# Half of the third exponential tile added in place by GpSimd, six key buffers with spread loads, and late tiles gated after head group six

## The chip, the cores and the metric

The kernel runs on one core of one Trainium2 chip. The metric is the device time of one execution in microseconds, lower being better. Inside the core five engines work side by side, each through its own instructions in order, held together by semaphores: TensorE (PE, matmuls; PEld is its weight load), VectorE (DVE), ScalarE (ACT), GpSimd (POOL) and SyncE (SP), which here issues nearly all DMA transfers. POOL issues a few transfers itself, and makes their descriptors in software.

## The reference

With `xn` the layer norm of `x` (2048 rows of 512, bfloat16), the result is `x + s * silu(b)`:

- `s` is attention with 32 heads of width 128 over given keys and values (2048 each): `q = xn @ wq`, `p = softmax(q @ k.T / sqrt(128))`, `o = p @ v`, and the heads' outputs side by side times `wo`.
- `b` is a two-layer mixer: gelu of a layer norm times `w1`, its quarters shifted by one or two rows, times `w2`, added to `xn`; then a gelu MLP of width 1792 over a second layer norm.

## The kernel before

A first stage (to about 118 us) does the layer norms, the mixer and half of its MLP; `silu(b)`, the **gate**, is kept in DRAM in tiles of 128 rows. The attention follows, and takes nearly all of the time.

The attention is cut into 128 **units**, numbered 0 to 127 here: one head for one block of 512 queries. The order is: head group `g` (eight groups of four heads), then query block `qt` (four), then head `hh` in the group. A group thus has 16 units; unit `16*g + 4*qt + hh`. A unit has eight **slots** `p`, numbered through as `n = 8*u + p`. In each slot (`s_slot`, L432) PE multiplies two chunks of 128 keys by the 512 queries into `ps_s`, and ACT takes the exponential of both (128 x 1024, L443) into half of a tile `pT`; a unit fills four such tiles, `pT[0]` to `pT[3]`. The product with the values (`pv_slot`, L475) comes 10 slots later. The rest of a unit is woven into the slots: query projections for units ahead (`product`, L374, in Strassen's form for pairs of units, finished by DVE in L420 to L428), and output projections (`wo_product`, L569, in Strassen's form for groups 1 to 5, `wo_mm`, L611, for the others).

The softmax's denominators are DVE's work. For unit `u`:

- slot 4: `add_first` (L449): `acc = pT[0] + pT[1]`, 128 x 2048, both inputs in SBUF.
- slot 6: for units in `APART` (L1046, units 24 to 109) POOL adds the two halves of `pT[2]` into a tile `ph` (`add_aside`, L455, 128 x 1024). For other units DVE adds the whole of `pT[2]` into `acc` (`add_next`, L465, 128 x 2048).
- slot 0 or 1 of the next unit: `add_last` (L1092): in `APART` DVE adds `ph` into the lower half of `acc` (`add_join`, L460), then in every unit `pT[3]` into `acc` (L465); two folds follow (L469, L473).
- slot 3 of the next unit: SP transposes the folded row block (`tT<-acc`, L498). One unit on, DVE sums it (L503) and takes the reciprocal (L509); SP writes that to DRAM (`dr<-rc`, L511) and reads it back on all partitions (`rb<-dr`, L515); DVE then scales the unit's output from PSUM by it (`oT`, L527), which frees the PSUM bank.

All of these transfers stand in SP's one queue with the loads. `load_k` (L140) loads a head's keys in four pieces of 512 keys by a transposing DMA (L145), `load_v` (L149) its values in two. There are five key buffers and five value buffers. `at(n, fn)` (L135) hangs a call on slot `n`; the main loop (L1123) runs what is due at the end of the slot. L985 to L994 set the loads of the next group's heads: with `b` the group's unit 12, key pieces go two to a unit, in slots 5 and 6, from unit `b - 2` to `b + 6`.

The output sums over heads stand in SBUF per tile of 128 rows, `sacc[t]` (16 tiles; `t // 4` is the query block). **Late** tiles are those of query blocks 2 and 3. In group 6 they are turned from sums of `wo` into sums of the final result: `gate_load` fetches the gate (L600), `y_scale` multiplies the sum by half the gate (L629, DVE, both inputs in SBUF), `y_add` adds `x` by an accumulating DMA on POOL's queue (L633). L1080 to L1085 hang these on units 104 to 111 (scale at slot 3, POOL's DMA at slot 5). From then on each product for a late tile is gated before it is added: `wo_post` (L646) makes `tm = 0.5 * ps * gate` (L655) and adds it (L658) in group 6; in group 7 `y_out` (L635) adds and writes. Tiles of blocks 0 and 1 are finished within `wo_post` (L662 to L669). `wo_join` (L593) folds a sum that Strassen's form kept apart into the tiles, L1078 sets when. DVE's order is the program's order: `pin` keeps it.

Of the kernel before, what the change touches and what calls it, by code (L numbers as in the profile page):

```python
# [17 lines left out]
def kernel(  # L18
# [15 lines left out]
    nc = tc.nc  # L34
    P = nc.NUM_PARTITIONS
# [3 lines left out]
    Sq, D = x2d.shape  # L39
    _, H, Sk, Dh = A_k_cache.shape  # L40
# [10 lines left out]
    HG = 4  # L51
# [83 lines left out]
    def at(n, fn):  # L135
        todo[n].append(fn)
# [3 lines left out]
    def load_k(h, pieces):  # L140
        w = Sk // KSPLIT
        for i in pieces:
            if i == 0:
                kTs[h] = kp.tile([P, Sk], BF16, name="kT")
            pin(nc.sync.dma_start(  # L145
                out=kTs[h][:, i * w:(i + 1) * w],
                in_=A_k_cache[0, h, i * w:(i + 1) * w, :], transpose=True))

    def load_v(h, halves):  # L149
        v = A_v_cache[0, h].rearrange("(i p j) d -> p i j d", p=P, j=KJ)  # L150
        for i in halves:
            if i == 0 and h == H - 1:
                vX[0] = vp.tile([P, KC, Dh + 2], BF16, tag="vb", name="vx")
                pin(nc.vector.memset(vX[0][:, :, Dh:Dh + 1], 1.0))
                vBs[h] = vX[0][:, :, 0:Dh]
            elif i == 0:
                vBs[h] = vp.tile([P, KC, Dh], BF16, tag="vb", name="vb")
            w = KSPLIT // 2
            dst = vBs[h].rearrange("p (i j) d -> p i j d", j=KJ)
            for ks in [slice(i * w, (i + 1) * w)] if h < H - 1 else range(i * w, (i + 1) * w):  # L160
                pin(nc.sync.dma_start(out=dst[:, ks], in_=v[:, ks]))

    def load_w(h, eng=nc.sync):
        wqs[h] = wqp.tile([P, DC, Dh], BF16, name="wq_h")
# [2 lines left out]
    vX = {}  # L167
# [281 lines left out]
        pin(nc.vector.tensor_tensor(  # L449
            out=s["acc"][:], in0=s["pT"][0][:], in1=s["pT"][1][:], op=ALU.add))  # L450

    def add_aside(u):
        s = st[u]
        s["ph"] = pS.tile([P, 2, 512], BF16, tag="tm", bufs=2, name="ph")
        pin(nc.gpsimd.tensor_tensor(  # L455
            out=s["ph"][:], in0=s["pT"][2][:, 0:2, :], in1=s["pT"][2][:, 2:4, :], op=ALU.add))

    def add_join(u):
        a = st[u]["acc"]
        pin(nc.vector.tensor_tensor(  # L460
            out=a[:, 0:2, :], in0=a[:, 0:2, :], in1=st[u].pop("ph")[:], op=ALU.add))

    def add_next(u, i):
        a = st[u]["acc"]
        pin(nc.vector.tensor_tensor(out=a[:], in0=a[:], in1=st[u]["pT"][i][:], op=ALU.add))  # L465
# [73 lines left out]
    def halves(x):  # L539
        return x.rearrange("p (a c) -> p a c", a=2)  # L540
# [87 lines left out]
    def y_scale(t):  # L628
        pin(nc.vector.scalar_tensor_tensor(  # L629
            out=sacc[t], in0=sacc[t], scalar=0.5, in1=halves(gin[t]), op0=ALU.mult, op1=ALU.mult))  # L630

    def y_add(t):
        pin(nc.gpsimd.dma_start(out=sacc[t], in_=halves(xsrc[t]), accum_op=ALU.add))  # L633

    def y_out(t, tm, queue):  # L635
        y = token(False, "y")
        pin(nc.vector.tensor_tensor(out=halves(y[:]), in0=halves(tm[:]), in1=sacc[t], op=ALU.add))
        pin(queue.dma_start(out=out2d[t * P:(t + 1) * P, :], in_=y[:]))

    owed = deque()  # L640
# [5 lines left out]
    def wo_post(g, t, n):  # L646
        ps = wo_box.pop(0)
        if g == 0:
            sa_open(t)
            pin(nc.vector.tensor_copy(out=sacc[t], in_=halves(ps[:])))  # L650
            return
        sa = sacc[t]
        if t // 4 in LATE:
            tm = pS.tile([P, D], FP32, tag="tm", bufs=2, name="tm")
            pin(nc.vector.scalar_tensor_tensor(  # L655
                out=tm[:], in0=ps[:], scalar=0.5, in1=gin[t], op0=ALU.mult, op1=ALU.mult))
            if g < NG - 1:
                pin(nc.vector.tensor_tensor(out=sa, in0=sa, in1=halves(tm[:]), op=ALU.add))  # L658
# [7 lines left out]
        pin(nc.vector.scalar_tensor_tensor(
            out=halves(gl), in0=sa, scalar=0.5, in1=halves(gl), op0=ALU.mult, op1=ALU.mult))
        pin(nc.vector.tensor_tensor(out=xl[:], in0=gl, in1=xl[:], op=ALU.add))
        pin(nc.sync.dma_start(out=out2d[t * P:(t + 1) * P, :], in_=xl[:]))  # L669

# [452 lines left out]
    for n in range(UB * SPU):  # L1123
# [234 lines left out]
```

## Time and profile before

| what | us |
|---|---|
| three runs | 1226.6, 1231.92, 1233.73 (median 1231.92) |
| the profiled execution | 1233.66 |
| its span, first to last instruction | 1231.9 |
| PE busy | 1214.8 |
| ACT busy | 1106.2 |
| DVE busy | 1087.9 |
| POOL busy | 244.2 |
| granted TensorE clock, mean | 0.999 |

What lies around the span is 1233.66 - 1231.9 = 1.76 us. Matmuls are pipelined in the profile, so a busy PE is not a PE at its peak; the windows of single units say more than the share of the whole. "Idle before, with releaser" in a timeline is the time that an engine stood still ahead of an instruction, and the instruction or transfer that ended it.

### The profile page before, as it was taken

How to read it: one execution, taken by the hardware profiler on the slowest of the kernel's cores; microseconds unless marked ns; L12 is line 12 of the kernel's file. 1: busy time of each engine (PE TensorE's matmuls, PEld its weight loads, DVE VectorE, ACT ScalarE, POOL GpSimd, SP SyncE). 2: the span in 40 equal slices, each digit the busy share in tenths (PEclk: the TensorE clock that was granted, in tenths of full speed). 3: DMA queues.
4: the chain of work that ended last, by engine and by line, in shares of the span. 5: the costliest groups of instructions: out<-in, count | busy, mean ns of one | idle time of the engine just before them, and what ended most of it. 6: DMA issues, size and time to landing. Idle time of an engine off the chain costs nothing.

```text
span 1231.9 us, 18553 instructions
## 1 busy us (share of the span) xinstructions
PE 1214.8 (99%) x6469; PEld 667.1 (54%) x6591; DVE 1087.9 (88%) x1891; ACT 1106.2 (90%) x1241; POOL 244.2 (20%) x185
## 2 busy tenths in 40 slices
PE   9999999999999999999999999999999999899998
PEld 7466444455555555555555555555555555455545
DVE  7853778999999999999989999999998899899997
ACT  6345999899999999999999999999999999899996
POOL 5300000000023222223223222223232333200000
PEclk9999999999999999999999999999999999999999
DMA  8671224454344523453244423552334345553432
GB/s 181 168 154 51 48 52 76 96 104 82 69 82 104 112 48 78 100 104 77 75 90 100 102 52 82 102 109 60 78 91 103 83 88 114 116 119 66 91 96 68
DMA packets 248157, 113.05 MB, mean 92 GB/s; under 512 B 195328, under 2 KB 231296, under 8 KB 248064
## 3 DMA queue, kind: packets, MB, share of 16 engines
q1 hardware_dynamic: 244560, 107.21, 41.2%
q0 software_dynamic: 2944, 4.20, 1.6%
q8 instruction: 51, 0.84, 0.3%
q14 instruction: 42, 0.34, 0.2%
q10 hardware_dynamic: 560, 0.46, 0.1%
HBM read 69.60 MB, written 4.45 MB: 60 GB/s over the span
## 4 chain that ended last, share of the span: by engine, by line
PE 83%; DVE 12%; DMA 3%; issue 2%; ACT 0%; POOL 0%; DVEq 0%
PE ps_s L112 35%; PE ps_o L112 31%; PE ps_q L112 7%; PE ps_wo L112 7%; PE ps_m L112 3%; DVE acc L465 2%; DVE acc L449 2%; DVE oT L527 1%; DVE sm L503 1%; DMA rb<-dr 1%; DMA dr<-rc 1%; DMA tT<-acc 1%; DVE acc L473 1%; DVE acc L469 1%; DVE sacc L658 0%
## 5 line engine op out<-in xcount | busy, mean ns | idle before, releaser
L443 ACT ACTIVATE pT<-ps_s 128x1024 bf16<-128x1024 f32 x1016 | 1015.6, 1028 | 56.3 <-PE ps_s L112 25.3
L112 PE MATMUL ps_s<-qT,kT 128*128 128x512 bf16 (+1 forms) x2057 | 608.4, 378 | 4.3 <-DVE qT L428 3.7
L112 PE MATMUL ps_o<-pT,vb 128*128 128x512 bf16 x1889 | 569.9, 379 | 4.4
L455 POOL TENSOR_TENSOR ph<-pT 128x1024 bf16<-128x1024 bf16 x86 | 200.2, 2328 | 625.8 <-ACT pT L443 600.8
L112 PEld LDWEIGHTS <-vb 128*128 128x128 bf16 x1984 | 193.8, 98 | 217.5 <-issue 1.5
L112 PEld LDWEIGHTS <-kT 128*128 128x128 bf16 x2064 | 230.8, 113 | 95.3 <-DVE qT L428 5.2
L465 DVE TENSOR_TENSOR acc<-acc,pT 128x2048 bf16<-128x2048 bf16 x168 | 204.4, 1217 | 19.5 <-ACT pT L443 13.6
L449 DVE TENSOR_TENSOR acc<-pT 128x2048 bf16<-128x2048 bf16 x127 | 157.6, 1241 | 11.3 <-ACT pT L443 11.2
L527 DVE TENSOR_TENSOR oT<-ps_o,rb 128x512 bf16<-128x512 f32 x127 | 86.7, 683 | 14.7 <-DMA rb<-dr 14.0
L591 DVE TENSOR_TENSOR sacc<-ps_wo,sacc 128x512 f32<-128x512 f32 (+1 forms) x160 | 97.0, 606 | 0.5 <-PE ps_wo L112 0.5
L112 PE MATMUL ps_wo<-wo_h,oT 128*128 128x512 bf16 (+1 forms) x330 | 91.7, 327 | 1.6 <-DVE tm L655 0.6
L503 DVE TENSOR_REDUCE sm<-tT 128x4 f32<-128x512 bf16 x124 | 84.0, 677 | 6.5 <-DMA tT<-acc 5.8
L469 DVE TENSOR_TENSOR acc<-acc 128x1024 bf16<-128x1024 bf16 x127 | 87.3, 687 | 2.5
L112 PEld LDWEIGHTS <-wc 128*128 128x128 bf16 x440 | 43.0, 98 | 52.5 <-issue 0.8
L112 PEld LDWEIGHTS <-oT 128*128 128x128 bf16 x448 | 43.5, 98 | 47.9 <-issue 0.9
L112 PEld LDWEIGHTS <-wq_h 128*128 128x128 bf16 x398 | 39.0, 98 | 46.7 <-issue 0.6
L112 PE MATMUL ps_q<-xnT,wq_h 128*128 128x256 bf16 (+1 forms) x284 | 60.3, 298 | 0.3
L460 DVE TENSOR_TENSOR acc<-acc,ph 128x1024 bf16<-128x1024 bf16 x86 | 58.6, 681 | 2.0 <-POOL ph L455 1.9
L298 ACT ACTIVATE h2T<-ps_s 128x1024 bf16<-128x1024 f32 x28 | 28.6, 1022 | 31.6 <-PE ps_s L112 31.6
L473 DVE TENSOR_TENSOR acc<-acc 128x512 bf16<-128x512 bf16 x127 | 53.4, 421 | 2.5
L112 PEld LDWEIGHTS <-so 128*128 128x128 bf16 x320 | 31.3, 98 | 38.6 <-issue 1.2
L112 PEld LDWEIGHTS <-w_sb 128*128 128x128 bf16 x368 | 33.6, 98 | 29.1
(134 smaller groups left out, 903.7 us busy)
## 6 DMA issues: line engine op xcount, KB each, us to landing
rb<-dr SPq DMA_DIRECT2D x127, 256.0 KB, 3.9
vb<-in_A_v_cache_dram SPq DMA_DIRECT2D x62, 256.0 KB, 3.0
wq_h<-in_A_wq_dram SPq DMA_DIRECT2D x32, 128.0 KB, 2.8
wo_h<-in_A_wo_dram SPq DMA_DIRECT2D x32, 128.0 KB, 2.3
w_sb<-in_B_w_dram SPq DMA_DIRECT2D x8, 256.0 KB, 4.7
kT<-in_A_k_cache_dram SPq DMA_TRANSPOSE x128, 2.7
gate<-xall POOLq DMA_DIRECT2D x16, 128.0 KB, 2.3
sacc<-in_A_x_dram POOLq DMA_DIRECT2D x8, 256.0 KB, 4.3
```

What stands on the lines that cost most here:

```text
L112: pin(nc.tensor.matmul(out=out, lhsT=lhsT, rhs=rhs, start=start, stop=stop, **kw))
L298: pin(nc.scalar.activation(out=h2[c][:, f], in_=ps[:], func=ACT.Gelu_apprx_tanh))
L443: pin(nc.scalar.activation(out=s["pT"][-1][:, jj:jj + 2, :], in_=sps[:], func=ACT.Exp, scale=SCALE))
L449: pin(nc.vector.tensor_tensor(out=s["acc"][:], in0=s["pT"][0][:], in1=s["pT"][1][:], op=ALU.add))
L455: pin(nc.gpsimd.tensor_tensor(out=s["ph"][:], in0=s["pT"][2][:, 0:2, :], in1=s["pT"][2][:, 2:4, :], op=ALU.add))
L460: pin(nc.vector.tensor_tensor(out=a[:, 0:2, :], in0=a[:, 0:2, :], in1=st[u].pop("ph")[:], op=ALU.add))
L465: pin(nc.vector.tensor_tensor(out=a[:], in0=a[:], in1=st[u]["pT"][i][:], op=ALU.add))
L469: pin(nc.vector.tensor_tensor(out=a[:, 0:2, :], in0=a[:, 0:2, :], in1=a[:, 2:4, :], op=ALU.add))
L473: pin(nc.vector.tensor_tensor(out=a[:, 0, :], in0=a[:, 0, :], in1=a[:, 1, :], op=ALU.add))
L503: pin(nc.vector.tensor_reduce(out=sm[:], in_=s["tT"][:], axis=mybir.AxisListType.X, op=ALU.add))
L527: pin(nc.vector.tensor_tensor(out=to, in0=o, in1=rb, op=ALU.mult))
L591: pin(nc.vector.tensor_tensor(out=out, in0=ps, in1=out, op=ALU.add))
```

## The change

It has these parts:

- **The third tile.** In `APART`, POOL adds the lower half of `pT[2]` straight into the lower half of `acc` (slot 6), and DVE adds the upper half into the upper half (in `add_last`). `ph` is gone. The shapes (128 x 1024) stay.
- **`APART`** now runs from unit 24 to 124.
- **Keys.** Heads with `h % 6 == 5` have a key buffer of their own (tag `kx`, in the place of `ph` and `tm`), so there are six. The pieces of the first head of a group are loaded one a unit from `b - 10`, those of the second from `b - 6`, those of the third and fourth from `b + 1` to `b + 6`. Values move up by one slot, those of a group's first head by one unit.
- **Late tiles.** Gate loads, scales and POOL's adds of `x` move from units 103 to 111 to units 112 to 121, one tile a unit; POOL's DMA now stands at slot 6, behind POOL's add. In group 6 a late tile's product is added plainly (one DVE instruction less for each of eight tiles). `tm` of group 7 takes a key buffer.
- **Order.** The last two steps of tiles of blocks 0 and 1 (`y_last`) wait for slot 3 of a next unit; four `wo_join` pairs move up by four to five units.

PE's instructions and their order stay as they are; DVE has eight instructions fewer.

```diff
-            if i == 0:
-                kTs[h] = kp.tile([P, Sk], BF16, name="kT")
+            if i == 0 and h % (HG + 2) == HG + 1:
+                kTs[h] = pS.tile([P, Sk], BF16, tag="kx", bufs=1, name="kT")
+            elif i == 0:
+                kTs[h] = kp.tile([P, Sk], BF16, tag="kT", name="kT")
...
-    def add_aside(u):
-        s = st[u]
-        s["ph"] = pS.tile([P, 2, 512], BF16, tag="tm", bufs=2, name="ph")
-        pin(nc.gpsimd.tensor_tensor(
-            out=s["ph"][:], in0=s["pT"][2][:, 0:2, :], in1=s["pT"][2][:, 2:4, :], op=ALU.add))
-
-    def add_join(u):
-        a = st[u]["acc"]
-        pin(nc.vector.tensor_tensor(
-            out=a[:, 0:2, :], in0=a[:, 0:2, :], in1=st[u].pop("ph")[:], op=ALU.add))
+    def add_half(u, eng, part):
+        a, e = st[u]["acc"], st[u]["pT"][2]
+        pin(eng.tensor_tensor(out=a[:, part, :], in0=a[:, part, :], in1=e[:, part, :], op=ALU.add))
...
-        if t // 4 in LATE:
-            tm = pS.tile([P, D], FP32, tag="tm", bufs=2, name="tm")
+        if t // 4 in LATE and g == NG - 1:
+            if t % 2 == 0:
+                pair[0] = kp.tile([P, 2, D], FP32, tag="kT", name="tm")
+            tm = pair[0][:, t % 2, :]
             pin(nc.vector.scalar_tensor_tensor(
-                out=tm[:], in0=ps[:], scalar=0.5, in1=gin[t], op0=ALU.mult, op1=ALU.mult))
-            if g < NG - 1:
-                pin(nc.vector.tensor_tensor(out=sa, in0=sa, in1=halves(tm[:]), op=ALU.add))
-            else:
-                owed.append((t, tm))
+                out=tm, in0=ps[:], scalar=0.5, in1=gin[t], op0=ALU.mult, op1=ALU.mult))
+            owed.append((t, tm))
             return
         pin(nc.vector.tensor_tensor(out=sa, in0=halves(ps[:]), in1=sa, op=ALU.add))
-        if g < NG - 1:
-            return
+        if g == NG - 1:
+            last.append(t)
...
-            for i in range(KSPLIT):
-                at((b - 2 + (2 * hh + i // 2 + (hh > 0))) * SPU + (5, 6)[i % 2], lambda h=h, i=i: load_k(h, (i,)))
+            for i, u in enumerate(((-10, -9, -8, -7), (-6, -5, -2, -1) if g else (-4, -3, -2, -1), (1, 1, 2, 3), (4, 5, 5, 6))[hh]):
+                at((b + u) * SPU + 5, lambda h=h, i=i: load_k(h, (i,)))
             for i in range(2):
-                at((b - 1 + (2 * hh + i + (hh > 0))) * SPU + 7, lambda h=h, i=i: load_v(h, (i,)))
+                at((b + (-2, 2, 4, 6)[hh] + i) * SPU + 6, lambda h=h, i=i: load_v(h, (i,)))
...
-    APART = range(FIRST + 2 * HG, (GY * QT + LATE[0]) * HG + 6)
+    APART = range(FIRST + 2 * HG, NU - 3)
...
-    for u, qt, i in ((6, 2, 0), (7, 2, 1), (8, 3, 0), (10, 3, 1), (16, 0, 0), (18, 0, 1), (20, 1, 0), (22, 1, 1)):
+    for u, qt, i in ((6, 2, 0), (7, 2, 1), (8, 3, 0), (10, 3, 1), (12, 0, 0), (14, 0, 1), (16, 1, 0), (17, 1, 1)):
         o_steps[(LATER + u) * SPU + 3].append((wo_join, qt, i))
-    for u, r, i in ((8, 0, 0), (9, 2, 1), (10, 1, 2), (11, 3, 3), (12, 4, 4), (13, 6, 6), (14, 5, 7), (15, 7, 5)):
-        n = (LATER + u) * SPU + 3
-        t = 4 * LATE[0] + r
-        at(max(n - 2 * SPU, (LATER + 7) * SPU + 1 + i), lambda t=t, i=i: gate_load(t, i))
-        at(n, lambda t=t: y_scale(t))
-        at(n + 2, lambda t=t: y_add(t))
+    for i in range(2 * HG):
+        n = (LATER + 18 + i) * SPU
+        t = 4 * LATE[0] + i
+        at(n - 2 * SPU + 4, lambda t=t, i=i: gate_load(t, i))
+        at(n + 3, lambda t=t: y_scale(t))
+        at(n + 6, lambda t=t: y_add(t))
...
         if u in APART:
-            add_join(u)
+            add_half(u, nc.vector, HI)
...
+        if p == 3 and last:
+            y_last(last.popleft())
         if p == 6:
-            add_aside(u) if u in APART else add_next(u, 2)
+            add_half(u, nc.gpsimd, LO) if u in APART else add_next(u, 2)
```

More of the change, by code (lines that the diff above doesn't have):

```diff
@@ L151, in load_v @@
         for i in halves:
[L152 to L156, printed above, removed]
+            if i == 0 and h < H - 1:
                 vBs[h] = vp.tile([P, KC, Dh], BF16, tag="vb", name="vb")
@@ L161, in load_v, with open_vx @@
                 pin(nc.sync.dma_start(out=dst[:, ks], in_=v[:, ks]))
+    def open_vx():
+        vX[0] = vp.tile([P, KC, Dh + 2], BF16, tag="vb", name="vx")
+        pin(nc.vector.memset(vX[0][:, :, Dh:Dh + 1], 1.0))
+        vBs[H - 1] = vX[0][:, :, 0:Dh]
     def load_w(h, eng=nc.sync):
@@ L636, in y_out @@
         y = token(False, "y")
-        pin(nc.vector.tensor_tensor(out=halves(y[:]), in0=halves(tm[:]), in1=sacc[t], op=ALU.add))
+        pin(nc.vector.tensor_tensor(out=halves(y[:]), in0=halves(tm), in1=sacc[t], op=ALU.add))
         pin(queue.dma_start(out=out2d[t * P:(t + 1) * P, :], in_=y[:]))
@@ L652, in wo_post, with y_last @@
         sa = sacc[t]
-        if t // 4 in LATE:
-            tm = pS.tile([P, D], FP32, tag="tm", bufs=2, name="tm")
+        if t // 4 in LATE and g == NG - 1:
+            if t % 2 == 0:
+                pair[0] = kp.tile([P, 2, D], FP32, tag="kT", name="tm")
+            tm = pair[0][:, t % 2, :]
             pin(nc.vector.scalar_tensor_tensor(
-                out=tm[:], in0=ps[:], scalar=0.5, in1=gin[t], op0=ALU.mult, op1=ALU.mult))
-            if g < NG - 1:
-                pin(nc.vector.tensor_tensor(out=sa, in0=sa, in1=halves(tm[:]), op=ALU.add))
-            else:
-                owed.append((t, tm))
+                out=tm, in0=ps[:], scalar=0.5, in1=gin[t], op0=ALU.mult, op1=ALU.mult))
+            owed.append((t, tm))
             return
         pin(nc.vector.tensor_tensor(out=sa, in0=halves(ps[:]), in1=sa, op=ALU.add))
-        if g < NG - 1:
-            return
+        if g == NG - 1:
+            last.append(t)
+    pair, last = {}, deque()
+    def y_last(t):
         xl, gl = fin.pop(t), gin[t]
         pin(nc.vector.scalar_tensor_tensor(
-            out=halves(gl), in0=sa, scalar=0.5, in1=halves(gl), op0=ALU.mult, op1=ALU.mult))
+            out=halves(gl), in0=sacc[t], scalar=0.5, in1=halves(gl), op0=ALU.mult, op1=ALU.mult))
         pin(nc.vector.tensor_tensor(out=xl[:], in0=gl, in1=xl[:], op=ALU.add))
@@ L988 @@
             h = (g + 1) * HG + hh
-            for i in range(KSPLIT):
-                at((b - 2 + (2 * hh + i // 2 + (hh > 0))) * SPU + (5, 6)[i % 2], lambda h=h, i=i: load_k(h, (i,)))
+            for i, u in enumerate(((-10, -9, -8, -7), (-6, -5, -2, -1) if g else (-4, -3, -2, -1), (1, 1, 2, 3), (4, 5, 5, 6))[hh]):
+                at((b + u) * SPU + 5, lambda h=h, i=i: load_k(h, (i,)))
             for i in range(2):
-                at((b - 1 + (2 * hh + i + (hh > 0))) * SPU + 7, lambda h=h, i=i: load_v(h, (i,)))
+                at((b + (-2, 2, 4, 6)[hh] + i) * SPU + 6, lambda h=h, i=i: load_v(h, (i,)))
+            if h == H - 1:
+                at((b + 6) * SPU + 3, open_vx)
             at((b + (-3, -3, 0, 0)[hh]) * SPU + (5, 7)[hh % 2], lambda h=h: load_w(h))
```

## The prediction

> **What bounds the kernel now.** I read the page first: busy times, the chain that ended last, the costliest groups.
>
> ```profile
> PE 1214.8 (99%) x6469; PEld 667.1 (54%) x6591; DVE 1087.9 (88%) x1891; ACT 1106.2 (90%) x1241; POOL 244.2 (20%) x185
> PE 83%; DVE 12%; DMA 3%; issue 2%; ACT 0%; POOL 0%; DVEq 0%
> L443 ACT ACTIVATE pT<-ps_s 128x1024 bf16<-128x1024 f32 x1016 | 1015.6, 1028 | 56.3 <-PE ps_s L112 25.3
> L455 POOL TENSOR_TENSOR ph<-pT 128x1024 bf16<-128x1024 bf16 x86 | 200.2, 2328 | 625.8 <-ACT pT L443 600.8
> L465 DVE TENSOR_TENSOR acc<-acc,pT 128x2048 bf16<-128x2048 bf16 x168 | 204.4, 1217 | 19.5 <-ACT pT L443 13.6
> L460 DVE TENSOR_TENSOR acc<-acc,ph 128x1024 bf16<-128x1024 bf16 x86 | 58.6, 681 | 2.0 <-POOL ph L455 1.9
> ```
>
> PE is the bound, and the change takes nothing from PE. What can be won is only time in which PE or ACT stands still; where that is, the shares don't say. So I cut the attention into stretches of whole units, by the starts of each unit's first exponential. In this windows view the first figure is the length, the x behind PEld the matmuls issued:
>
> ```profile
> 599.69:607.91 8.22, 8.17 (x45) 4.53 (x45) 7.94 (x15) 8.16 (x11) 2.35 (x2) 1.00 0.30 80
> 607.91:616.56 8.65, 8.60 (x49) 4.91 (x49) 7.61 (x13) 8.18 (x10) 2.26 (x2) 1.00 0.31 78
> 532.11:937.68 405.57, 403.24 (x2167) 226.31 (x2209) 374.21 (x661) 391.95 (x433) 111.82 (x49) 1.00 0.41 87
> 937.68:981.58 43.90, 42.64 (x226) 23.24 (x229) 38.23 (x67) 40.88 (x47) 13.33 (x6) 1.00 0.46 97
> 1050.59:1099.54 48.95, 44.60 (x214) 22.53 (x217) 45.93 (x72) 41.07 (x46) 5.60 (x5) 0.97 0.57 116
> 1099.54:1107.97 8.43, 8.38 (x43) 4.35 (x43) 8.22 (x14) 8.26 (x12) 0.00 (x0) 1.00 0.52 111
> 1107.97:1116.62 8.65, 8.60 (x45) 4.54 (x45) 8.55 (x15) 8.07 (x10) 0.00 (x0) 1.00 0.44 103
> 1150.84:1159.73 8.89, 8.53 (x43) 4.33 (x43) 8.61 (x14) 8.26 (x11) 0.00 (x0) 1.00 0.39 88
> ```
>
> The first two rows are an undisturbed pair of units in groups 1 to 5: 8.22 us, which is eight exponentials of 1028 ns, and 8.65 us, in which PE is busy but for 0.05: 16.87 together. Rows six and seven are such a pair in group 7: 8.43 + 8.65 = 17.08. Against these, the other rows show what is lost:
>
> - Units 109 to 113 (48.95): two pairs and an odd unit would be 2 x 17.08 + 8.65 = 42.81. **Lost 6.14.**
> - Units 96 to 100 (43.90): 2 x 16.87 + 8.22 = 41.96. **Lost 1.94.**
> - Unit 120 (8.89 against 8.43): lost 0.46.
> - Groups 3 to 5 together (405.57): 24 pairs are 404.88. Lost 0.69.
>
> In all 9.23 us. Everything else runs at its floor, so this is about all that the change can win in the attention, and I go by where each loss comes from.
>
> **The large loss: a port held by GpSimd.** These are timeline rows of POOL, DVE and PE (start, length, engine, line; idle before in brackets):
>
> ```profile
> 1057.35 1.08 POOL L633 DMA_DIRECT2D sacc<-in_A_x_dram  x1 [6.55 <-DVE wc L372]
> 1058.12 2.46 POOL L455 TENSOR_TENSOR ph<-pT 128x1024 bf16<-128x1024 bf16 x1
> ...
> 1057.58 4.10 DVE L449 TENSOR_TENSOR acc<-pT 128x2048 bf16<-128x2048 bf16 x1
> 1061.60 0.68 DVE L428 TENSOR_TENSOR qT<-ps_q,tq 128x512 bf16<-128x512 f32 x1
> ...
> 1062.33 1.04 PE L112 MATMUL ps_s<-qT,kT 128*128 128x512 bf16 x2 [3.48 <-DVE qT L428]
> ...
> 1078.49 1.08 POOL L633 DMA_DIRECT2D sacc<-in_A_x_dram  x1 [8.61 <-DVE wc L372]
> ...
> 1078.64 1.22 DVE L449 TENSOR_TENSOR acc<-pT 128x2048 bf16<-128x2048 bf16 x1
> ```
>
> `add_first` took 4.10 instead of 1.22 us. It ended at 1061.68, 1.10 after POOL's add ended (1060.58): DVE seems to have got its inputs only then. Next in DVE's queue was the copy of the queries (L428), and PE waited 3.48 us for it; the rest of the 6.14 is DVE catching up. The last two rows show the same DVE instruction beside the same POOL DMA without an add behind it: 1.22 us, no harm. So it takes a DMA with an add behind it in POOL's queue, both while DVE starts an instruction with two inputs in SBUF. The reverse order is seen all the time:
>
> ```profile
> 613.04 1.22 DVE L449 TENSOR_TENSOR acc<-pT 128x2048 bf16<-128x2048 bf16 x1
> 614.36 2.12 POOL L455 TENSOR_TENSOR ph<-pT 128x1024 bf16<-128x1024 bf16 x1 [6.31 <-ACT pT L443]
> ...
> 970.33 1.22 DVE L449 TENSOR_TENSOR acc<-pT 128x2048 bf16<-128x2048 bf16 x1
> 970.42 3.11 POOL L455 TENSOR_TENSOR ph<-pT 128x1024 bf16<-128x1024 bf16 x1 [6.41 <-DVE so L566]
> ```
>
> POOL's add takes 2.12 us behind `add_first` and 3.11 when it starts beside it, longer by most of the overlap (to 971.55, so 1.13). The Trainium skill ("SBUF — State Buffer", section "Who interferes with whom") says that DVE and GpSimd share a port pair, that a DVE instruction with two SBUF inputs contends with a GpSimd instruction that reads SBUF, and that whichever starts first holds the pair while the other blocks; the rows above agree with it, in both directions.
>
> **The change, part by part.**
>
> *POOL's half in units 24 to 109.* Same shapes: 681 ns on DVE (L460 row), 2.12 us on POOL. New is that POOL must wait for `add_first`. By the rows above it was shut out until `add_first` ended anyhow, so its end moves by a semaphore's delay, about the 0.10 us between 614.26 and 614.36 above. Of DVE's two instructions behind it only the second (L465) now needs POOL, 0.68 us later than the first, which covers that. I price this at 0. If the cover failed (DVE's half shut out until POOL ends), DVE's waits for POOL, 1.9 us in all in the L460 row, might double: 1.9 us at worst. It can't gain, since these units are at the floor.
>
> *POOL's half in units 110 to 124.* Each swaps a DVE add of 1217 ns for one of 681 ns: 15 x 0.536 = 8.0 us of DVE. None of it is on PE's path directly; it is what lets DVE catch up. Between `add_first` and its half DVE has only instructions with at most one SBUF input: query parts, sums and `oT` from PSUM, and L503; the steps with two (joins, scales, `y_last`) now stand at slot 3, ahead of `add_first`.
>
> *Late tiles.* Durations are in this lines view (count | busy, mean ns):
>
> ```profile
> L629 DVE SCALAR_TENSOR_TENSOR sacc<-sacc,gin 128x512 f32<-128x512 f32 x8 | 5.5, 684 | 0.0
> L658 DVE TENSOR_TENSOR sacc<-sacc,tm 128x512 f32<-128x512 f32 x4 | 2.8, 691 | 0.1
> ```
>
> Eight L658-like adds go: 8 x 0.69 = 5.5 us of DVE in units 111 to 118. Eight scales of 0.68 leave units 104 to 111 and come back in 114 to 121. In units 118 to 121 scale and swap together give DVE -0.54 + 0.68 = +0.14 us a unit; unit 115 has 8.55 of 8.65 busy now (windows), so these four are full, but start without a backlog. POOL's eight DMAs move behind its add, and the next add comes a unit later, so the pattern of 1057 is gone. With it goes the 6.14. In its place POOL's add is late by nothing: the scale that the DMA waits for is ahead of `add_first`, on which the add before it waits already. The eight gate loads now share SP with key loads in three units and are needed two units later.
>
> *Keys.* These are issue-to-landing medians, first in a quiet stretch (697 to 733), then in 925 to 972:
>
> ```profile
> tT<-acc SPq DMA_TRANSPOSE x5, 2.4
> dr<-rc SPq DMA_DIRECT2D x4, 2.0 KB, 1.6
> ...
> kT<-in_A_k_cache_dram SPq DMA_TRANSPOSE x10, 2.8
> tT<-acc SPq DMA_TRANSPOSE x6, 3.5
> dr<-rc SPq DMA_DIRECT2D x5, 2.0 KB, 3.4
> ```
>
> And from the timeline of SP and DVE in the second stretch:
>
> ```profile
> 943.91 1.24 SPq L498 DMA_TRANSPOSE tT<-acc  x1
> 945.20 2.56 SPq L145 DMA_TRANSPOSE kT<-in_A_k_cache_dram  x2
> ...
> 947.16 0.69 DVE L527 TENSOR_TENSOR oT<-ps_o,rb 128x512 bf16<-128x512 f32 x1 [2.27 <-DMA rb<-dr]
> ```
>
> Two key pieces hold SP for 2.56 us, and the denominators' chain behind them gets 1.1 (tT) and 1.8 us (dr) longer; DVE waited 2.27 us for its end, then PE for DVE. After the change SP's order has two pieces in 3 units of a group, where it had 8, and one in 10. One piece issued in slot 5 lands after 2.8 us, about when the next `dr` goes out. SP's queue carries as many transfers as before. I take three quarters of the 1.94 (1.46) and half of the 0.69 (0.35); the ends are 0 and all of it.
>
> *Order at the end.* The two instructions of `y_last`, in the lines of 1150 to 1168:
>
> ```profile
> L666 DVE SCALAR_TENSOR_TENSOR gl<-sacc,gl 128x512 bf16<-128x512 f32 x2 | 1.4, 691 | 0.1
> L668 DVE TENSOR_TENSOR xl<-gl,xl 128x512 bf16<-128x512 bf16 x2 | 0.8, 425 | 0.1
> ```
>
> They come up to a unit later, and `oT` no longer stands behind them: I take it that this ends unit 120's 0.46. The last pair falls into unit 126 and costs nothing while DVE is ahead of PE; bound 0.69 + 0.43 = 1.1 us.
>
> Sum: 6.14 + 1.46 + 0.46 + 0.35 = 8.4 us. Against the profiled execution (1233.66, of which 1231.9 is span) this gives **1225.3 us**. The median of the runs shown is 1231.92, so it is 0.5% below that. The fastest run shown, 1226.6, is 7.06 below the profiled execution: as if it had lacked the stall of 1057; I can't see it, but it fits.
>
> **The rivals.**
>
> 1. *The key loads win nothing.* For: groups 3 to 5 had the same bunches and lost only 0.69 in 405 us. Against: SP's rows. Then 8.4 - 1.8 = 6.6 are won: **1227.1**.
> 2. *The hold by GpSimd comes back once*, in units 110 to 121, where POOL now has both an add and a DMA in a unit. By the Trainium skill's rule (same section) the add alone would hold out a two-input DVE instruction. Price by the row: one such stall with its aftermath, 6.14: **1231.4**. Or DVE, full in units 118 to 121, waits for POOL there; four units at half an add each (0.5) give 2.0, **1227.3**.
> 3. *It comes back often, and the kernel is slower.* The place is POOL's queue in units 114 to 121, where eight DMAs stand between adds. If the scale is late, a DMA slides to just before the next unit's add, the order of 1057. One costs 6.14, so from the second on the gain is gone; three give 1225.3 + 18.4 = **1243.7**. Against it: the scale is ahead of the add that the DMA follows.
> 4. *The change does nothing*, since the stall of 1057 is a chance event: against a run without it only 2.3 us are won. That is the same time, 1225.3, beside a faster kernel before.
>
> **How the numbers follow.** Forecast 1225.3 (own range 1224.2 to 1226.6): 0.68. Rival 1, with the small form of rival 2: 0.15. One stall: 0.10. Several: 0.07. The low end is all 9.23 won, 1224.4, less 1.2 (a seventh of DVE's 8.0 us, should the last units gain by its lead): 1223.2. The high end is the forecast with the bounds 1.9, 1.1 and half of the key loads' 1.8 unwon, 1229.2, rounded up to 1230; it leaves out the stalls (0.17). A difference of about 0.5% is what a measurement of this kernel can tell from no change; that is 6.2 us, or 1225.8. The forecast lies just beyond it: of its 0.68, 0.50 are faster by more, and 0.18 within. Rival 1 and the single stall are within: same 0.43, slower 0.07, faster 0.50.
>
> **What would show it.** Right: no L449 over 1.3 us; PE's wait for L428 gone; units 109 to 113 in some 43 us, 96 to 100 in some 42.5; POOL's 101 adds at 2.1 us each, started just behind `add_first`. Wrong: a long DVE instruction beside a POOL DMA; odd units of 118 to 121 well over 8.65; L465 waiting for POOL in many units; `oT` still waiting over 1 us for `rb`.

## The result, and the profile after

| | us, median (lowest to highest) | runs |
|---|---|---|
| before | 1232.26 (1226.6 to 1233.73) | 7 |
| after | 1225.38 (1225.03 to 1225.72) | 7 |

The ratio is 0.9948, with a 95% interval of 0.9932 to 0.9965 (ratios here are of means): 0.5% faster. The profiled execution of the kernel after took 1225.03 us, its span 1223.3. The medians lie 6.9 us apart; the two profiled executions, of before one as slow as its slowest and of after its fastest, 8.6. In three later sessions before ranged from 1227.27 to 1241.57 us (34 executions), and after, run in two of them, from 1224.61 to 1226.96 (9 executions, ratios 0.9921 and 0.9938). The kernel after is thus the steadier one too.

From the page of the kernel after, first the busy times and the chain, then the costliest groups (busy us, mean ns of one | idle time ahead, and what ended it). The code has moved by a few lines: the exponential is now L446, `add_first` L452, both halves of the third tile L457, `add_next` L461, `oT` L523, the copy of the queries L431, the scale L625.

```profile
PE 1217.8 (100%) x6591; PEld 666.8 (55%) x6591; DVE 1069.6 (87%) x1883; ACT 1105.8 (90%) x1241; POOL 258.4 (21%) x200
PE 93%; DVE 5%; DMA 1%; issue 1%; POOL 0%; ACT 0%; DVEq 0%; POOLq 0%
L457 POOL TENSOR_TENSOR acc<-acc,pT 128x1024 bf16<-128x1024 bf16 x101 | 214.6, 2125 | 766.9 <-DVE acc L452 506.1
L461 DVE TENSOR_TENSOR acc<-acc,pT 128x2048 bf16<-128x2048 bf16 x153 | 186.3, 1218 | 20.5 <-ACT pT L446 13.1
L523 DVE TENSOR_TENSOR oT<-ps_o,rb 128x512 bf16<-128x512 f32 x127 | 86.3, 680 | 2.6 <-DMA rb<-dr 1.9
L457 DVE TENSOR_TENSOR acc<-acc,pT 128x1024 bf16<-128x1024 bf16 x101 | 68.6, 679 | 0.0
```

DVE's and DMA's shares of the chain fell from 12 and 3% to 5 and 1%. POOL's add has a mean of 2125 ns where it had 2328, and most of its wait is now ended by `add_first`. DVE's half never waits (0.0).

The windows by units, as shown of before: units 56 and 57, groups 3 to 5, units 96 to 100, 109 to 113, 114, 115, 119, 120, 121. Behind the length stand the busy times of PE, PEld, DVE, ACT and POOL with their instructions, then the granted clock, the share of the DMA engines and GB/s.

```profile
599.51:607.76 8.25, 8.25 (x46) 4.58 (x45) 8.01 (x16) 8.18 (x10) 2.77 (x2) 1.00 0.50 110
607.76:616.38 8.62, 8.62 (x50) 4.88 (x49) 7.41 (x13) 8.16 (x9) 2.13 (x1) 1.00 0.30 78
531.94:936.92 404.98, 404.98 (x2210) 226.55 (x2209) 373.04 (x661) 391.89 (x432) 102.05 (x49) 1.00 0.40 87
936.92:979.19 42.27, 42.19 (x230) 23.39 (x229) 38.30 (x68) 40.86 (x47) 11.06 (x6) 1.00 0.55 100
1048.20:1091.05 42.85, 42.85 (x218) 22.31 (x217) 38.63 (x70) 40.66 (x45) 10.25 (x6) 1.00 0.40 90
1091.05:1099.50 8.45, 8.45 (x44) 4.37 (x43) 7.13 (x14) 8.28 (x11) 2.90 (x3) 1.00 0.56 127
1099.50:1108.12 8.62, 8.62 (x46) 4.52 (x45) 7.86 (x14) 8.08 (x9) 2.79 (x2) 1.00 0.62 132
1133.64:1142.62 8.98, 8.80 (x46) 4.43 (x45) 8.31 (x15) 8.18 (x10) 1.88 (x2) 1.00 0.56 122
1142.62:1151.08 8.46, 8.46 (x44) 4.38 (x43) 8.22 (x14) 8.29 (x11) 2.88 (x3) 1.00 0.54 125
1151.08:1160.05 8.97, 8.79 (x46) 4.42 (x45) 8.71 (x16) 8.18 (x9) 3.40 (x3) 1.00 0.54 129
```

The floor stayed (8.25 + 8.62 = 16.87; in group 7 8.45 + 8.62 = 17.07). Units 109 to 113 fell from 48.95 to 42.85, 96 to 100 from 43.90 to 42.27, unit 120 from 8.89 to 8.46. But 121 is 8.97, where it was 8.64, and 119 8.98, where it was 8.71. This table has the stretches for the main kernels, from the starts of each unit's first exponential, in one profiled execution of each (what the experiments are follows below; the profiled execution of a_half is the slowest of its seven):

| units | before | after | a_half | b_late | b_both | b_keys | b_apart | c_even |
|---|---|---|---|---|---|---|---|---|
| 48-95 | 405.56 | 404.98 | 406.54 | 405.90 | 406.45 | 406.18 | 404.98 | 405.00 |
| 96-100 | 43.90 | 42.26 | 44.36 | 42.40 | 43.23 | 42.61 | 42.21 | 42.07 |
| 109-113 | 48.95 | 42.85 | 45.22 | 42.89 | 42.87 | 42.87 | 42.85 | 42.87 |
| 118-121 | 34.67 | 34.86 | 34.66 | 34.98 | 35.65 | 34.86 | 35.63 | 34.14 |
| 122-126 | 42.73 | 42.40 | 42.73 | 43.68 | 42.68 | 42.40 | 42.67 | 42.40 |
| span | 1231.9 | 1223.3 | 1229.9 | 1225.5 | 1226.7 | 1225.7 | 1225.0 | 1223.0 |

### The profile page after: what moved, and what is told of

The parts are those of the page before. It is cut to its first block, busy times and chain, and to the rows that moved or that the text cites. A ratio compares the mean times of both kernels' runs of the same rounds, so it can differ in the third digit from the quotient of the medians.

```text
span 1223.3 us, 18718 instructions
## 1 busy us (share of the span) xinstructions
PE 1217.8 (100%) x6591; PEld 666.8 (55%) x6591; DVE 1069.6 (87%) x1883; ACT 1105.8 (90%) x1241; POOL 258.4 (21%) x200
## 4 chain that ended last, share of the span: by engine, by line
PE 93%; DVE 5%; DMA 1%; issue 1%; POOL 0%; ACT 0%; DVEq 0%; POOLq 0%
PE ps_s L112 39%; PE ps_o L112 36%; PE ps_q L112 8%; PE ps_wo L112 8%; PE ps_m L112 3%; DVE acc L461 1%; DVE acc L452 1%; DMA rb<-dr 0%; DMA tT<-acc 0%; DVE acc L465 0%; DVE sm L499 0%; DMA xin<-in_A_x_dram 0%; DVE acc L469 0%; PE ps_oh L112 0%; DVE qT L431 0%
## 5 line engine op out<-in xcount | busy, mean ns | idle before, releaser
L446 ACT ACTIVATE pT<-ps_s 128x1024 bf16<-128x1024 f32 x1016 | 1015.4, 1028 | 48.3 <-PE ps_s L112 17.4
L112 PE MATMUL ps_o<-pT,vb 128*128 128x512 bf16 x1984 | 589.9, 379 | 0.0
L457 POOL TENSOR_TENSOR acc<-acc,pT 128x1024 bf16<-128x1024 bf16 x101 | 214.6, 2125 | 766.9 <-DVE acc L452 506.1
L461 DVE TENSOR_TENSOR acc<-acc,pT 128x2048 bf16<-128x2048 bf16 x153 | 186.3, 1218 | 20.5 <-ACT pT L446 13.1
L452 DVE TENSOR_TENSOR acc<-pT 128x2048 bf16<-128x2048 bf16 x127 | 154.6, 1217 | 11.3 <-ACT pT L446 11.3
L523 DVE TENSOR_TENSOR oT<-ps_o,rb 128x512 bf16<-128x512 f32 x127 | 86.3, 680 | 2.6 <-DMA rb<-dr 1.9
L457 DVE TENSOR_TENSOR acc<-acc,pT 128x1024 bf16<-128x1024 bf16 x101 | 68.6, 679 | 0.0
L426 DVE TENSOR_TENSOR tq<-ps_q,tq 128x256 f32<-128x256 f32 x55 | 23.3, 423 | 33.7 <-PE ps_q L112 33.6
```

Source lines behind the costliest of these rows:

```text
L112: pin(nc.tensor.matmul(out=out, lhsT=lhsT, rhs=rhs, start=start, stop=stop, **kw))
L426: pin(nc.vector.tensor_tensor(out=s["u3"][:], in0=ps[:, 0], in1=s["u"][:], op=ALU.add))
L446: pin(nc.scalar.activation(out=s["pT"][-1][:, jj:jj + 2, :], in_=sps[:], func=ACT.Exp, scale=SCALE))
L452: pin(nc.vector.tensor_tensor(out=s["acc"][:], in0=s["pT"][0][:], in1=s["pT"][1][:], op=ALU.add))
L457: pin(eng.tensor_tensor(out=a[:, part, :], in0=a[:, part, :], in1=e[:, part, :], op=ALU.add))
L523: pin(nc.vector.tensor_tensor(out=to, in0=o, in1=rb, op=ALU.mult))
```

## The experiments

Theory A, the prediction's: the long `add_first` needs a POOL DMA with POOL's add queued behind it. Rival B: POOL's add alone does it, whenever it starts ahead of a late `add_first`. The runs were made in three sessions, each beside the kernel before: a_order, a_half, b_keys and b_apart in the first (median of before 1235.61), d_swap, b_both and c_early in the second (1234.82), b_late, b_dmafirst and c_even in the third (1232.95). The kernel after ran again in the second and the third. Ratios are to before in the same session.

**a_order**: before, with POOL's DMA behind POOL's add.

```diff
-        at(n + 2, lambda t=t: y_add(t))
+        at(n + 3, lambda t=t: y_add(t))
```

> The kernel before, with POOL's accumulating DMA one slot later, behind POOL's add of the same unit instead of ahead of it; nothing else. Port theory (a DMA with an add right behind it in POOL's queue takes the port from add_first): the 4.10 us add_first is gone, units 109 to 113 fall from 48.95 to some 43 us, time 1226 to 1228. Rival, DVE overload (the scales and the two-step late tiles on a full DVE make the stall): nothing moves, 1231 to 1234.

Measured: 1235.7 us (1231.73 to 1237.2), ratio 0.9989 [0.9971, 1.0007]: no gain. The timeline of POOL and DVE at unit 109 (start, length):

```profile
1056.80 2.17 POOL L455 TENSOR_TENSOR ph<-pT 128x1024 bf16<-128x1024 bf16 x1 [6.15 <-ACT pT L443]
1058.91 1.08 POOL L633 DMA_DIRECT2D sacc<-in_A_x_dram  x1
...
1056.90 3.14 DVE L449 TENSOR_TENSOR acc<-pT 128x2048 bf16<-128x2048 bf16 x1
```

The DMA now comes last, and `add_first` is still held: it took 3.14 and ended 1.07 after POOL's add (1058.97). **Theory A falls**: the add alone, 0.10 us ahead of `add_first`, is enough.

**d_swap**: before, with `add_first` of units 40, 56 and 72 put about a slot later, so that POOL's add starts first, far from any POOL DMA.

```diff
+                if u - 1 in (40, 56, 72):
+                    add_first(u - 1)
...
-            add_first(u)
+            if u not in (40, 56, 72):
+                add_first(u)
```

> The kernel before, with add_first of units 40, 56 and 72 put later in DVE's order, behind the row sum of the unit before, so that POOL's add (which doesn't wait for it here) starts first; there is no DMA of POOL near any of the three. Port theory: each of the three takes about 2.4 to 3.3 us, ending 1.1 us after POOL's add. Rival, a DMA of POOL is needed for the hold: 1.22 us each. Beside these the kernel keeps its own stall at unit 109.

Measured: 1239.15 us in one run. POOL and DVE in unit 40, and in unit 63, where nothing was moved:

```profile
470.99 2.12 POOL L455 TENSOR_TENSOR ph<-pT 128x1024 bf16<-128x1024 bf16 x1 [5.87 <-ACT pT L443]
...
472.13 2.06 DVE L449 TENSOR_TENSOR acc<-pT 128x2048 bf16<-128x2048 bf16 x1
...
665.76 2.14 POOL L455 TENSOR_TENSOR ph<-pT 128x1024 bf16<-128x1024 bf16 x1 [6.31 <-ACT pT L443]
...
665.84 3.14 DVE L449 TENSOR_TENSOR acc<-pT 128x2048 bf16<-128x2048 bf16 x1
```

Units 56 and 72 show 1.95 and 2.09 us, less than the 2.4 to 3.3 expected, since POOL's add had started over 1.1 us earlier. In each case `add_first` ends 1.08 us after POOL's add, which is nearly its whole work. Unit 63 was an unplanned case: POOL's add 0.08 us ahead, 3.14 us for `add_first`, and a unit of 11.11 us where 8.65 is the floor. So B holds, and in the kernel before it can strike any unit of `APART` whose `add_first` is late.

The trace of before itself shows what decides. The first four rows are of unit 104, where POOL's DMA stands ahead of `add_first` and POOL's add behind the DMA, as in unit 109. The last row is the exponential in unit 109 that completes `pT[2]`, the input of POOL's add:

```profile
1012.74 1.02 ACT L443 ACTIVATE pT<-ps_s 128x1024 bf16<-128x1024 f32 x1
1012.89 1.17 POOL L633 DMA_DIRECT2D sacc<-in_A_x_dram  x1 [5.44 <-DMA rb<-dr]
1013.10 1.22 DVE L449 TENSOR_TENSOR acc<-pT 128x2048 bf16<-128x2048 bf16 x1
1013.91 2.40 POOL L455 TENSOR_TENSOR ph<-pT 128x1024 bf16<-128x1024 bf16 x1
...
1056.29 1.02 ACT L443 ACTIVATE pT<-ps_s 128x1024 bf16<-128x1024 f32 x1 [0.20 <-PE ps_s L112]
```

In unit 104 `pT[2]` is complete at 1013.76, 0.66 us after `add_first` has started, and `add_first` takes its 1.22: there a DMA with an add behind it does no harm. In unit 109 `pT[2]` is complete at 1057.31, 0.26 us before `add_first` starts, and `add_first` is held; in a_order, without the DMA ahead, it is the same 0.26. The four kernels with `ph` (before, a_order, d_swap, b_late) have 344 such units. `add_first` is held in the seven where `pT[2]` was complete at least 0.16 us before it started, and in none of the 337 others, where that was at most 0.05 us. So what counts is whether POOL's add has its input before a late `add_first` starts.

**a_half**: before, with only the half added in place (units 24 to 109), so that POOL's add waits for `add_first`.

```diff
-            add_join(u)
+            add_half(u, nc.vector, HI)
...
-            add_aside(u) if u in APART else add_next(u, 2)
+            add_half(u, nc.gpsimd, LO) if u in APART else add_next(u, 2)
```

> The kernel before, with only POOL's half added in place in units 24 to 109, so that POOL's add waits for add_first; DMA order, key loads, late tiles and the end of APART as before. Port theory: an add that waits for add_first can't take the port from it, so the stall goes here too, 1226 to 1228. Rival, order theory (only the place of the DMA counts): the DMA is still ahead of the add, the stall stays, 1231 to 1234. Rival, overload: 1231 to 1234.

Measured: 1229.91 us (1228.72 to 1231.65), ratio 0.9945 [0.9917, 0.9973]. No add is held, also where `pT[2]` was complete first (by 0.51 us in unit 63 and by 0.26 in 109; `add_first` took 1.22 in both). But 109 to 113 are still 45.22, 2.4 above the floor. DVE and PE in unit 109, which starts at 1052.33 (idle before in brackets):

```profile
1052.51 0.69 DVE L520 TENSOR_TENSOR oT<-ps_o,rb 128x512 bf16<-128x512 f32 x1 [0.87 <-DMA rb<-dr]
1054.29 0.69 DVE L496 TENSOR_REDUCE sm<-tT 128x4 f32<-128x512 bf16 x1 [1.09 <-DMA tT<-acc]
1059.75 1.22 DVE L449 TENSOR_TENSOR acc<-pT 128x2048 bf16<-128x2048 bf16 x1
...
1057.62 0.38 PE L112 MATMUL ps_q<-xnT,wc 128*128 128x256 bf16 x2 [0.44 <-DVE qT L425]
1061.62 0.62 PE L112 MATMUL ps_s<-qT,kT 128*128 128x512 bf16 x2 [0.60 <-DVE qT L428]
```

DVE itself is late: `add_first` starts 7.42 us into the unit. The hold was only a part of the loss, and the 1226 to 1228 expected were not reached.

**b_late**: before, with only the late tiles moved as in the kernel after (with the four joins; the half still goes to a tile of its own).

```diff
-        if t // 4 in LATE:
+        if t // 4 in LATE and g == NG - 1:
...
+    for i in range(2 * HG):
+        n = (LATER + 18 + i) * SPU
+        t = 4 * LATE[0] + i
+        at(n - 2 * SPU + 4, lambda t=t, i=i: gate_load(t, i))
+        at(n + 3, lambda t=t: y_scale(t))
+        at(n + 6, lambda t=t: y_add(t))
```

> The kernel before with only the late tiles moved as in the kernel after (gate loads, scales and POOL's DMAs at units 112 to 121, plain adds of the products in group 6, the four joins earlier); POOL's add still goes to a tile of its own and waits for nothing of DVE's, and DVE adds the whole third tile from unit 110 on. Theory (the late tiles make DVE late in units 104 to 111, and a late add_first meets POOL's add): without them add_first is in time in unit 109, no long L449 there, and 109 to 113 fall from 48.95 to about 43; units 118 to 121, with a full add and a scale each, grow by 0.3 to 0.7 us a unit. In all 3 to 5 us shorter than the kernel before. Rival (the hold needs only POOL's add free to start, wherever DVE is): a long L449 still comes in 109 or near, 109 to 113 stay above 46, and the time stays within 2 us of the kernel before.

Measured: 1227.23 us (1226.44 to 1227.56), ratio 0.9952 [0.9939, 0.9966]. Unit 109 starts at 1049.01; DVE and POOL there:

```profile
1054.47 1.22 DVE L449 TENSOR_TENSOR acc<-pT 128x2048 bf16<-128x2048 bf16 x1
...
1055.67 2.13 POOL L455 TENSOR_TENSOR ph<-pT 128x1024 bf16<-128x1024 bf16 x1 [6.52 <-ACT pT L443]
```

`add_first` starts 5.46 us into the unit, where before had 6.99 (1057.58 - 1050.59), and ends as POOL's add starts (1055.69 and 1055.67). Units 109 to 113 fall to 42.89: **the late tiles alone take the whole loss away**. The gain is in the first of these windows (109 to 113), the price in the second (122):

```profile
1049.01:1091.90 42.89, 42.68 (x214) 22.29 (x217) 40.23 (x69) 40.63 (x45) 2.28 (x2) 1.00 0.46 102
1161.02:1170.40 9.38, 8.60 (x43) 4.38 (x43) 9.10 (x15) 8.32 (x11) 0.00 (x0) 1.00 0.51 111
```

DVE, with the whole third tile from unit 110 on and a scale in each unit from 114 to 121, ends behind: unit 122 takes 9.38 us, with DVE busy for 9.10 of it.

**b_keys**, **b_apart**, **b_both**: after, with the old load times of keys and values (the lines of the values are not shown); with `APART` ending at unit 109 again; with both.

```diff
-            for i, u in enumerate(((-10, -9, -8, -7), (-6, -5, -2, -1) if g else (-4, -3, -2, -1), (1, 1, 2, 3), (4, 5, 5, 6))[hh]):
-                at((b + u) * SPU + 5, lambda h=h, i=i: load_k(h, (i,)))
+            for i in range(KSPLIT):
+                at((b - 2 + (2 * hh + i // 2 + (hh > 0))) * SPU + (5, 6)[i % 2], lambda h=h, i=i: load_k(h, (i,)))
...
-    APART = range(FIRST + 2 * HG, NU - 3)
+    APART = range(FIRST + 2 * HG, (GY * QT + LATE[0]) * HG + 6)
```

> The changed kernel with the old times of the key and value loads (two key pieces to a unit). Forecast's view: 1.6 us lost again around units 96 to 100 and 0.6 us in groups 3 to 5, so 1227.3 to 1227.9. Rival, key loads win nothing: 1225.0 to 1225.7.

> The changed kernel with APART ending at unit 109 again, so that DVE adds the whole third tile in units 110 to 124 (8.0 us more of DVE). Port theory: the large stall stays away; DVE is over-full only in units 118 to 121 (scale and y_last), one to two us in all: 1226 to 1227.5. Rival, DVE's relief won the large part: 1230 to 1232.

> The changed kernel with the old key and value times and with APART ending at 109: what stays is the half in place and the late tiles behind group six. If the two undone parts add up (+2.4 and +1.8 of span so far): 1228 to 1230. Port theory: no add of 128 x 2048 on DVE over 1.3 us, units 109 to 113 at 43 to 44 us, so the late tiles are what took the second half of the large loss. Rival: the key loads make DVE late at unit 109, and with them back the units 109 to 113 stay at 45 us or more.

Measured: b_keys 1227.72 us (1226.58 to 1228.11), ratio 0.9925 [0.9901, 0.9949]; b_apart 1226.66 (1226.4 to 1227.42), 0.9919 [0.9895, 0.9943]; b_both 1228.51 (1227.8 to 1230.36), 0.9942 [0.9923, 0.9961]. In all three 109 to 113 stay at 42.9. Without the extended `APART`, 118 to 126 lose 1.04 us (35.63 + 42.67 against 34.86 + 42.40): unit 121 takes 9.78. With the old key loads the loss is elsewhere than I had it: 96 to 100 are 42.61, and unit 66, which starts at 685.07, takes 8.99 instead of 8.25. SP and DVE ahead of it:

```profile
674.29 2.55 SPq L147 DMA_TRANSPOSE kT<-in_A_k_cache_dram  x2
676.94 0.53 SPq L159 DMA_DIRECT2D vb<-in_A_v_cache_dram  x1
677.57 0.42 SPq L507 DMA_DIRECT2D dr<-rc  x1
681.57 0.32 SPq L511 DMA_DIRECT2D rb<-dr  x1
...
685.01 0.69 DVE L523 TENSOR_TENSOR oT<-ps_o,rb 128x512 bf16<-128x512 f32 x1 [1.64 <-DMA rb<-dr]
```

`dr` goes out behind two key pieces, and 4.00 us pass until `rb` can follow. It is the wait for `rb` that I had read at 947 of before, in another unit. But there I had taken the wrong pieces: those of 945.20 went out behind `rb` (943.54). The two that delay `dr` stand ahead of it:

```profile
935.57 2.55 SPq L145 DMA_TRANSPOSE kT<-in_A_k_cache_dram  x2
...
939.66 0.40 SPq L511 DMA_DIRECT2D dr<-rc  x1
943.54 0.32 SPq L515 DMA_DIRECT2D rb<-dr  x1
```

Over units 48 to 100 of before, the time from the issue of `dr` to that of `rb` has a median of 1.57 us in the 25 units with no key piece between the `rb` before and `dr`, and of 2.54 in the 28 with two. In after it is 1.42 (9 units), 1.59 with one piece (33 units) and 2.53 with two (11 units). DVE's waits for `rb` sum to 10.0 to 18.4 us over the trace in the six kernels with the old loads named next, and to 1.9 to 5.8 in the seven with the new ones.

Which unit loses differs between executions: 97 is 9.77 in before but 8.65 in a_order and b_late, which have the same loads; 66 is 8.22 in before and 8.98 in b_late. So I take units 48 to 100 as a whole: with the old loads 447.81 to 450.90 (six executions: before, a_order, a_half, b_late, b_keys, b_both; mean 449.2; d_swap is left out, since it moves `add_first` there), with the new ones 447.06 to 447.82 (seven; mean 447.4). The spread loads are worth about **1.7 us** in the mean; the lowest of the six (a_order) lies within the range of the seven.

**b_dmafirst**: after, with POOL's DMA at slot 5, ahead of POOL's add.

```diff
-        at(n + 6, lambda t=t: y_add(t))
+        at(n + 5, lambda t=t: y_add(t))
```

> The kernel after, with POOL's accumulating DMA of the late tiles at slot 5, ahead of POOL's add in its queue, the order that the kernel before has at 1057. If it is a DMA with an add behind it that holds out add_first (the prediction's reason), the long add_first comes back in some of units 114 to 121 and the time is about 6 us longer. If it is POOL's add started ahead of a late add_first (what the two runs without such a DMA showed), nothing is held out, since POOL's add now waits for add_first: no L452 over 1.3 us, 114 to 121 within 0.5 us of the kernel after, the time within 0.5 us.

Measured: 1225.35 us (1225.12 to 1225.9), as long as after. POOL and DVE in unit 119:

```profile
1140.51 1.08 POOL L629 DMA_DIRECT2D sacc<-in_A_x_dram  x1 [7.01 <-DVE sacc L625]
1141.49 2.26 POOL L457 TENSOR_TENSOR acc<-acc,pT 128x1024 bf16<-128x1024 bf16 x1
...
1140.13 1.22 DVE L452 TENSOR_TENSOR acc<-pT 128x2048 bf16<-128x2048 bf16 x1
```

A DMA with an add behind it, and `add_first` takes its 1.22. But the DMA, which waits for the scale, starts 0.38 to 0.69 us after `add_first` in all eight units, not ahead of it as at 1057, so this run alone says little of that order. Unit 109 of a_half has it: the DMA starts at 1059.52, 0.23 us ahead of `add_first`, the add behind it waits for `add_first`, and nothing is held.

**c_early** and **c_even**: after, with the eight scales (and their loads and DMAs) two units earlier; and with none in units 119 and 121.

```diff
-        n = (LATER + 18 + i) * SPU
+        n = (LATER + 16 + i) * SPU
...
+        n = (LATER + (18, 18, 19, 20, 20, 21, 22, 24)[i]) * SPU
```

> The changed kernel with the late tiles gated two units earlier (units 112 to 119, loads from 110), so that no scale shares units 120 and 121 with the last steps of the first tiles. If DVE is over-full there (units 119 and 121 take 8.98 where 8.62 is the floor), 0.3 to 0.7 us are won: 1224.6 to 1225.0 where the changed kernel shows 1225.4. If those units are long for another cause: no change.

> The kernel after, with the scales of the eight late tiles at units 114, 114, 115, 116, 116, 117, 118 and 120 where it has one a unit from 114 to 121, so that the odd units 119 and 121, in which the kernel after lost 0.27 and 0.34 us against the kernel before, have no scale (their gate loads and POOL's accumulating DMAs move along). Theory (in these units DVE, not PE, sets the length: the scale ahead of add_first makes the copy of the queries late): units 119 and 121 come back to 8.62, 118 to 121 fall from 34.86 to about 34.2, the time falls by 0.6 us against a kernel after of the same chip. Rival (any place for the scales costs the same, since DVE is short over the whole stretch): units 114 and 116, now with two scales each, grow by what 119 and 121 lose, and the time stays within 0.2 us.

> The changed kernel once more, as the partner of the others of this call on the same chip: 1225.0 to 1225.8, no DVE add over 1.3 us but the half of unit 120.

> The kernel after once more, unchanged, beside the other three on the same chip: 1225.4 to 1226.0 us, units 109 to 113 in 42.9, 118 to 121 in 34.9 us.

The two runs of after itself, after_again beside c_early and after_third beside c_even, gave 1225.94 us (1225.67 to 1226.96) and 1225.56 (1224.61 to 1225.68). c_early: 1226.27 (1225.96 to 1226.8), no gain: unit 121 is 8.62 again, but 113 (where a `wo_join` stands too) grows to 8.92, and 119, which still has a scale, stays at 8.98. c_even: **1224.63** (1224.21 to 1224.98), ratio to before 0.9932 [0.992, 0.9945], 0.9 us below after_third. In the kernel after, this is DVE in unit 121, and PE behind it:

```profile
1155.81 0.68 DVE L665 SCALAR_TENSOR_TENSOR gl<-sacc,gl 128x512 bf16<-128x512 f32 x1
1156.53 0.42 DVE L667 TENSOR_TENSOR xl<-gl,xl 128x512 bf16<-128x512 bf16 x1
1156.87 0.68 DVE L625 SCALAR_TENSOR_TENSOR sacc<-sacc,gin 128x512 f32<-128x512 f32 x1
1157.47 1.22 DVE L452 TENSOR_TENSOR acc<-pT 128x2048 bf16<-128x2048 bf16 x1
1158.61 0.68 DVE L431 TENSOR_TENSOR qT<-ps_q,tq 128x512 bf16<-128x512 f32 x1
...
1159.35 0.62 PE L112 MATMUL ps_s<-qT,kT 128*128 128x512 bf16 x2 [0.18 <-DVE qT L431]
```

The windows of units 119 to 121 in c_even, to be set against 8.98, 8.46 and 8.97:

```profile
1134.17:1142.79 8.62, 8.57 (x45) 4.52 (x45) 7.95 (x14) 8.08 (x9) 2.25 (x2) 1.00 0.56 118
1142.79:1151.24 8.45, 8.40 (x43) 4.36 (x43) 8.21 (x15) 8.28 (x11) 1.86 (x2) 1.00 0.47 101
1151.24:1159.86 8.62, 8.57 (x45) 4.53 (x45) 8.13 (x14) 8.08 (x10) 3.40 (x3) 1.00 0.50 115
```

Both odd units are back at their floor, and units 114 and 116, with two scales each, did not grow (114 to 117: 34.14 in both). c_even beats both kernels.

Not tried: the spread key loads alone on the kernel before; the sixth buffer stands in the place of `ph` and `tm`, which that kernel needs.

## Why the prediction was right, point by point

The forecast of 1225.3 met 1225.4, and the profiled execution (1225.03) won 8.63 us where the sum had 8.4. That it came so near is partly luck: unit 120's term of 0.46 came out as a loss of 0.19, and 0.41 more than counted from the keys and 0.33 not counted made up for it. The terms, each against the windows:

- **The large loss, 6.14: right in size (6.10), half right in its cause.** The step that failed is "So it takes a DMA with an add behind it in POOL's queue". It takes no DMA: a_order and d_swap show POOL's add alone holding `add_first`, from a start 0.08 us ahead on. So moving the DMAs behind the add ("the pattern of 1057 is gone. With it goes the 6.14") is not what won it: a_order does just that, and wins nothing. That the 6.14 went all the same is owed to other parts of the change. The Trainium skill ("SBUF — State Buffer", section "Who interferes with whom") says just this, that whoever issues first gets the shared port pair and the other blocks. The runs agree with it: `add_first` ends 1.07 to 1.09 us after POOL's add in all seven cases, and POOL's add had its input first in each, though in two of them its row shows the later start (see the end). I had used the rule as a rival and not as the cause. My counterexample, the harmless DMA at 1078, had no add near it, so it told the DMA apart from the pair, but never the pair from the add; unit 104, with the pair and no harm, stood in the same trace.
- **Which part wins it: not separated in the prediction, and two parts do.** The half in place, with its wait for `add_first`, removes the hold (a_half: 3.7 of the 6.1), where the prediction said that it "can't gain". The late tiles remove DVE's lateness, without which the hold doesn't come in 109 (b_late: all of it). In after the late tiles would do it alone. b_late and b_both both have the old loads and `APART` to 109, and b_both has the half in place as well (and the order of `y_last`): it was 2.6 us slower than after in its session, b_late 1.7 in its own. So no run shows that the half in place wins anything more once the late tiles are moved; it keeps a late `add_first` from being held in any unit.
- **The half at no cost: right.** DVE's half waits 0.0 us in all. Held by POOL, the other half of rival 2, it was once, for 0.21 us, and not 2.0 (in the other runs with the extended `APART` at most twice, by at most 0.37):

```profile
1150.12 2.12 POOL L457 TENSOR_TENSOR acc<-acc,pT 128x1024 bf16<-128x1024 bf16 x1 [5.58 <-ACT qT L415]
...
1151.89 0.89 DVE L457 TENSOR_TENSOR acc<-acc,pT 128x1024 bf16<-128x1024 bf16 x1
```

- **Keys, 1.46 + 0.35 = 1.81: right in size (1.7 over units 48 to 100), wrong in its shares.** That 96 to 100 lost 1.94 was in part that execution's draw: with the old loads they take 42.40 to 44.36, and the means of the six and the seven executions differ by 0.9 there and by 0.9 in 48 to 95. The rows that I read at 945.20 were also not those that cause the wait. In the profiled pair the two terms won 1.64 + 0.58. Rival 1 falls.
- **Unit 120, 0.46: mis-sized.** The unit came to its floor (8.46), but `y_last` now stands with a scale ahead of `add_first` in units 119 and 121, which lost 0.27 + 0.34. Units 118 to 121 lost 0.19 together. "Full, but start without a backlog" was right for 114 to 117 and wrong here: the two steps of `y_last`, 0.68 + 0.42 in the rows of 1155.81, were counted as moved, and not added to the unit that they moved to. c_even, without a scale in these units, wins 0.72 there.
- **Not counted:** 0.33 in units 122 to 126. Part of DVE's relief from the extended `APART` comes back at the end (b_apart loses 1.04 over 118 to 126).
- **Rivals 2 and 3**, a hold in the stretch with eight DMAs: no L452 is over 1.3 us. POOL's add now waits for `add_first`, whatever stands ahead of it in its queue (a_half, b_dmafirst).
- **Rival 4**, chance: in part true. All four profiles with before's late tiles (before, a_order, a_half, d_swap) have DVE late in 109, so that loss is no accident; but the hold at 665.84 in d_swap came unplanned, and before ranges over 1226.6 to 1233.73 and after over 0.69 us in the runs of the result. Which part of the loss the fastest runs of before lack, no trace shows.

## What to carry to other kernels

When two engines share a port, let the slower one's instruction wait by a data dependence for the one that matters: adding in place made POOL's add wait for `add_first`, and no `add_first` was held any more. When a step is moved into a unit, add up everything that now stands there ahead of the instruction that PE waits for, and leave the full units empty of it (c_even). Where one bunch of transfers loses time in one execution, take the loss over the whole stretch and the mean of several executions: the place moves, and the sum varies too (447.81 to 450.90 with the old loads).

## What the runs showed of the hardware

- A held DVE instruction seems to do nearly all of its work after the release: 1.07 to 1.08 us of 1.22 for 128 x 2048 (a_order, d_swap), and 0.54 of 0.68 for 128 x 1024 (after, 1152.24 to 1152.78). A start 0.08 us too late cost 1.92 us (3.14 instead of 1.22).
- One thing stays open. At 1057 of before, and again at 1062 of d_swap, the row of POOL's add shows a start 0.54 us *after* that of `add_first`, and `add_first` was held for 4.10 us instead of 3.14. There POOL's DMA had started 0.23 us ahead of `add_first`, and the add, with its input complete 0.26 us ahead, stood behind the DMA; in a_order the same lead of 0.26 gave 3.14 without the DMA. A DMA ahead may thus lengthen a hold. That it is needed is excluded; why the row of the add shows the later start was not found.
